# A norm, local-attention and shifted-MLP kernel on one core: p in bands of 32 queries by 48 keys, two weight loads on another queue, and a new operation order

## The chip, the cores and the metric

The kernel runs on one core of a Trainium2 chip. Its engines run side by side, each through its own list of instructions, and wait for one another by semaphores: TensorE (PE in the profile; its weight loads are listed as PEld), VectorE (DVE), ScalarE (ACT), GpSimd (POOL) and SyncE (SP). SP issues nearly all DMA transfers, and in this kernel it does little else. The metric is the device time of one execution in microseconds (us).

## The reference

x is 2048 tokens by 448 channels in bf16. The first half is attention with a window: 16 heads of 28 channels, and each query sees 8 keys, those at distance 0, 2, 4, ... 14 behind it.

```python
idx = pos[:, None] - off[None, :]          # off = 0, 2, ..., 14
logits = einsum("bhsd,bhswd->bhsw", q, k[idx]) * scale   # masked where idx < 0
attn = softmax(logits)
o = einsum("bhsw,bhswd->bhsd", attn, v[idx])
h = x + (o reshaped to 2048 x 448) @ wo    # q, k, v from layernorm(x) @ wqkv
```

The second half takes y = LN(h), where LN stands for layernorm: g = gelu(LN(y) @ w1); the four quarters of g's channels are shifted by -1, +1, -2 and +2 tokens; x1 = y + shifted @ w2. The output is h + x1 + gelu(LN(x1) @ w3) @ w4, where w3 is 448 x 1792 and w4 is 1792 x 448.

## The kernel before, in words

**Tiles.** The 2048 tokens are worked in four blocks t of 512 tokens for the attention and the first part of the MLP, and then in five units of 2, 4, 4, 4 and 2 tiles of 128 tokens (UNITS, L855) for the rest. The phases of a block are:

- N1 and A1: layernorm of x, the transpose of the normalised tokens into actT (channels on partitions), and the matmuls for q and k. PSUM (the tile ps) is copied to SBUF, to the tile arena.
- V: v by matmuls, copied to vt. Then DMA copies on SP build vw, the windows of v: each window is a range of 64 keys and the 16 before them, 80 rows, since a band of 64 queries reaches 14 keys back. The 16 columns of padding and the overlap are why vw is a second copy.
- A2: the products of q with each of its 8 keys, on DVE, into qk_r (128 x 4096, and 128 x 2048 for the last channels). TensorE sums them over each head's channels by matmuls with a matrix of ones, zc.
- Softmax: maximum (mx), difference (ls), exponential, sum, and the product pb, all of it on DVE and ACT. Two bands of the exponentials' 8 keys stand 80 columns apart in pb, and TensorE turns pb (matmuls with ident) into pt, keys on partitions.
- A3 (L781): for each il (128 queries) DVE spreads pt over a band matrix bd_r by a multiplication with a mask of zeros and ones (bmask), 80 partitions by 2048. TensorE multiplies it with vw: 32 matmuls per il, one for each head and half, whose weights are 80 rows by 32 columns of vw and whose moving side is 64 columns of bd_r. They lie in four column groups of the array (j). The result is copied to actT. Then follow the matmuls with wo and the residual.
- B1: the layernorm, a transpose of lntm into actT by DMA (an instruction DMA_TRANSPOSE on SP), the matmuls with w1, gelu.

Per unit there follow B2 (w2 and the residual, by scalar_tensor_tensor into arena), a layernorm with a DMA transpose, W3 (14 pairs of matmul sums with gelu into h3T) and B3 (w4, and the store).

**Order.** The program is first recorded as some 860 numbered operations. The table ORDER (L19) is one sequence of them all: each engine gets its operations in the order of this table, and buffers (pools bank, ln, act, qk, bd, h3) are handed out along it. The table OTHER (L50) lists the operations that go to their second choice of engine: a copy from ACT to DVE, or the product pb from DVE to POOL. `arrange` (L191) also keeps the two kinds of DMA apart: a DMA transpose waits for every plain copy that stands ahead of it in the sequence and behind the last transpose, and a plain copy waits for the transposes ahead of it. So SP's list is made of groups: copies, a transpose, copies, a transpose. All instructions are emitted from one line (L986 before; L1032 after), so the profile tells them apart by the names of their tiles: `actT<-lntm` on SP is a DMA transpose, `vw<-vt` a window copy.

**Loads.** x comes in seven transfers, the weights of q and k in two of 448 KB (load_rows, L426, into arena), v's in two of 224 KB, w3 in two of 896 KB, and w4 in two of 784 KB (L941). w4 takes the arena's place of wqkv, and so can be loaded only when TensorE has made the last use of wqkv. wqkv's and x's loads are the first things on SP's list.

Of the kernel before, what the change touches and what calls it, by code (L numbers as in the profile page):

```python
# [6 lines left out]
ALU = mybir.AluOpType  # L7
AX = mybir.AxisListType
# [40 lines left out]
"""  # L49
OTHER = """  # L50
92 102 187 188 381 493 499 502 505 549 550
"""
FULL = (4,)
FILL = (0, 0, 0, 0)
# [226 lines left out]
def bass_sequential_preLN__sliding_local_dilated__mixer_s_mlp__prompt_kernel(  # L281
# [7 lines left out]
    NTL = SEQ // 128  # L289
    NF = F // 128  # L290
    PADK = 16
    KW = 80
    KVW = PADK + 512
    SCALE = float(DH) ** -0.5
    EPS = 1e-5
    x2 = A_x.rearrange("b s d -> (b s) d")
    o2 = out.rearrange("b s d -> (b s) d")
    S = _Sched()
# [729 lines left out]
```

## Time and profile before

| | us |
|---|---|
| three runs | 192.14, 193.64, 194.31 |
| median | 193.64 |
| span of the profiled execution | 189.9 |
| median of the runs less that span | 3.7 |
| PE busy | 178.4 (94%), 2434 matmuls |
| DVE busy | 127.4 (67%), 226 instructions |
| ACT busy | 126.5 (67%), 295 instructions |
| POOL busy | 26.9 (14%) |
| DMA | 17.96 MB, 39.7% of 16 engines' span |

The span is the profiled execution's time from its first instruction to its last. The page gives no other time for that execution; what lies around the span (the launch and the end) is read from the runs, whose median is 3.7 us above it. PE's busy time is modelled from starts, so "busy" there doesn't mean that the array runs at its peak. The TensorE clock that was granted is 1.00 in every stretch.

### The profile page before, as it was taken

To read this page: it belongs to the slowest core of one execution; us is meant where nothing else is said; L and a number is where in the kernel's file an instruction comes from. 1 tells how busy PE (TensorE), PEld (TensorE's weight loads), DVE (VectorE), ACT (ScalarE), POOL (GpSimd) and SP (SyncE) were. 2 spreads that over 40 slices of the span, in tenths; PEclk is the share of its full clock that TensorE was granted. 3 is DMA by queue.
4 is the path that set the end of the run, shared out by engine and by line. 5 is a ranking of instruction groups with operands and counts; after the bars stand their busy time and mean duration, and the time that the engine had idled before them with its cause. 6 is when DMAs were issued, how large, how long until landed. Compare 5 with 4: busy or idle time off the path is not lost.

```text
span 189.9 us, 5626 instructions
## 1 busy us (share of the span) xinstructions
PE 178.4 (94%) x2434; PEld 107.5 (57%) x2434; DVE 127.4 (67%) x226; ACT 126.5 (67%) x295; POOL 26.9 (14%) x62
## 2 busy tenths in 40 slices
PE   6799989999988668999999999999999999999994
PEld 2494334545443434486544666666545664699973
DVE  6799999999999999897795337673973024001322
ACT  3569999999998999977698677049167004740330
POOL 2340000000002100202910000008026304000000
DMA  5993065554961553663534200518008202300202
GB/s 138 358 281 85 16 112 128 114 131 102 308 202 28 96 114 93 136 159 88 114 66 85 53 3 0 106 34 183 4 0 91 23 0 77 79 3 0 74 28 73
DMA packets 33217, 17.96 MB, mean 95 GB/s; under 512 B 21944, under 2 KB 32680, under 8 KB 33192
## 3 DMA queue, kind: packets, MB, share of 16 engines
q1 hardware_dynamic: 33192, 17.60, 39.7%
q8 instruction: 19, 0.31, 0.7%
q14 instruction: 6, 0.05, 0.1%
HBM read 7.91 MB, written 1.84 MB: 51 GB/s over the span
## 4 chain that ended last, share of the span: by engine, by line
PE 62%; DVE 17%; ACT 11%; DMA 6%; SPq 1%; issue 1%
PE ps L986 62%; DVE qk_r L986 9%; ACT arena L986 3%; DMA xin<-in_A_x_dram 3%; DMA actT<-lntm 3%; DVE bd_r L986 3%; ACT lntm L986 3%; ACT actT L986 2%; ACT vt L986 2%; DVE lntm L986 1%; DVE mx L986 1%; DVE st L986 1%; SPq L986 1%; ACT xin L986 1%; DVE pb L986 1%
## 5 line engine op out<-in xcount | busy, mean ns | idle before, releaser
L986 PE MATMUL ps<-actT,arena 64*128 64x512 bf16 (+1 forms) x756 | 68.8, 329 | 1.3 <-ACT vt L986 1.0
L986 PEld LDWEIGHTS ps<-actT,arena 64*128 64x128 bf16 x756 | 38.6, 94 | 27.3 <-ACT vt L986 2.6
L986 ACT ACTIVATE h3T<-ps 128x512 bf16<-128x512 f32 (+1 forms) x70 | 31.1, 515 | 33.7 <-PE ps L986 33.0
L986 PE MATMUL ps<-arena,h3T 64*128 64x448 bf16 (+2 forms) x434 | 44.5, 343 | 0.0
L986 PEld LDWEIGHTS ps<-arena,h3T 64*128 64x128 bf16 (+1 forms) x434 | 31.2, 94 | 11.5 <-ACT h3T L986 0.2
L986 DVE SCALAR_TENSOR_TENSOR qk_r<-ps,mrs,arena 128x448 bf16<-128x448 f32 (+1 forms) x17 | 10.6, 652 | 40.3 <-PE ps L986 33.2
L986 ACT ACTIVATE arena<-ps 128x512 bf16<-128x512 f32 (+6 forms) x73 | 32.8, 495 | 5.2 <-PE ps L986 4.6
L986 DVE TENSOR_TENSOR qk_r<-arena 128x4096 bf16<-128x4096 bf16 (+1 forms) x16 | 31.9, 2016 | 0.3 <-ACT arena L986 0.3
L986 POOL TENSOR_TENSOR arena<-arena,xin 128x448 f32<-128x448 f32 x16 | 16.7, 1066 | 43.5 <-DVE lntm L986 43.5
L986 DVE TENSOR_TENSOR bd_r<-arena,bmask 80x2048 bf16<-80x2048 bf16 x16 | 19.1, 1216 | 0.2 <-ACT arena L986 0.2
L986 PE MATMUL ps<-actT,w_s 64*112 64x512 bf16 x112 | 13.6, 378 | 2.2 <-DMA actT<-lntm 2.2
L986 PE MATMUL ps<-wo_s,actT 64*128 64x448 bf16 x128 | 14.8, 350 | 0.8 <-issue 0.5
L986 PE MATMUL ps<-w_s,arena 64*128 64x448 bf16 (+1 forms) x128 | 13.9, 350 | 1.0 <-ACT arena L986 1.0
L986 DVE SCALAR_TENSOR_TENSOR arena<-xin,rs_y,ps 128x448 f32<-128x448 bf16 x16 | 10.3, 676 | 4.0 <-PE ps L986 3.9
L986 PE MATMUL ps<-arena,actT 64*128 64x448 bf16 x112 | 12.5, 350 | 0.1
L986 ACT ACTIVATE lntm<-xin,nm 128x448 bf16<-128x448 bf16 x16 | 10.6, 685 | 2.2 <-DVE nm L986 2.0
L986 ACT ACTIVATE rs_x<-mv,epsilon 128x4 f32<-128x4 f32 (+2 forms) x16 | 4.9, 306 | 10.7 <-DVE mv L986 10.5
L986 ACT ACTIVATE actT<-ps 128x512 bf16<-128x512 f32 (+2 forms) x18 | 10.9, 644 | 1.4 <-PE ps L986 1.2
L986 PEld LDWEIGHTS ps<-actT,w_s 64*112 64x112 bf16 x112 | 7.7, 127 | 7.2 <-ACT arena L986 1.6
L986 PEld LDWEIGHTS ps<-w_s,arena 64*128 64x128 bf16 (+1 forms) x128 | 7.2, 94 | 6.1 <-ACT arena L986 1.1
L986 DVE BATCH_NORM_STATS2 st<-xin 128x6 f32<-128x448 bf16 x16 | 9.1, 616 | 1.7 <-DMA xin<-in_A_x_dram 1.4
L986 PEld LDWEIGHTS ps<-wo_s,actT 64*128 64x128 bf16 x128 | 6.2, 94 | 6.0 <-issue 0.9
(72 smaller groups left out, 156.6 us busy)
## 6 DMA issues: line engine op xcount, KB each, us to landing
arena<-in_B_w_dram SPq DMA_DIRECT2D x2, 896.0 KB, 8.1
out_dram<-qk_r SPq DMA_DIRECT2D x15, 112.0 KB, 1.9
arena<-in_B_w_dram SPq DMA_DIRECT2D x2, 784.0 KB, 5.2
vw<-vt SPq DMA_DIRECT2D x4, 320.0 KB, 5.7
vw<-vt SPq DMA_DIRECT2D x4, 256.0 KB, 3.9
arena<-in_A_wqkv_dram SPq DMA_DIRECT2D x2, 448.0 KB, 4.6
xin<-in_A_x_dram SPq DMA_DIRECT2D x2, 448.0 KB, 8.5
xin<-in_A_x_dram SPq DMA_DIRECT2D x3, 224.0 KB, 6.0
```

The source lines that it names most:

```text
L986: inst = getattr(eng, meth)(**kw)
```

## The change

1. **Bands.** With NARROW = (0, 1, 2, 3), all four blocks use bands of 32 queries by 48 keys. The mask is nmask (112 partitions, 16 columns), the product of the softmax is pn (windows 128 columns apart), the turn writes 112 rows: 48 keys of one half window, 16 rows unused, and 48 keys of the other half. bd_r is 112 partitions by 1024 for each il in place of 80 by 2048. The matmuls with vw become 64 per il in place of 32; each has 48 rows by 32 columns of weights and 32 moving columns, in two row groups and four column groups of the array, and writes one of two PSUM banks. Two il share the two banks, and two copies per pair of il bring them to actT (16 copies in all, as before).
2. **Windows of v.** vw has 128 partitions, and each block needs vwa (128 KB), vwd, vwb and vwe (192 KB each), vwc (48 KB) and vwp (16 KB, not for block 0): 768 KB in six copies, where it was 640 KB in four. In all 23 copies stand where 15 stood.
3. **Weights.** The two 448 KB loads of q's and k's weights are issued by ACT's queue instead of SP's. w3 is loaded in four pieces of 448 KB, and w4 in four (458, 458, 344 and 344 KB).
4. **Order.** ORDER is a new sequence throughout, and OTHER has 21 entries instead of 11. On the ACT engine 16 loads of an activation table stand where there were 12.

```diff
 FULL = (4,)
+NARROW = (0, 1, 2, 3)
...
-        load_rows("wqk", wqkv_s[:, :, 0:2 * D], A_wqkv, 0, 2 * D)
+        load_rows("wqk", wqkv_s[:, :, 0:2 * D], A_wqkv, 0, 2 * D, "act")
...
-        load_rows("w3", w3_s, B_w3, 0, F)
+        for q in range(2):
+            load_rows("w3%d" % q, w3_s[:, :, q * 896:q * 896 + 896], B_w3, q * 896, 896)
...
+            if narrow:
+                dma("vwa%d" % sl, vw[PADK:NK, sl, 0:8:2, :], vt[0:32, sl, :, :], 32 * 4096)
+                dma("vwd%d" % sl, vw[64:64 + NK, sl, 0:8:2, :], vt[16:64, sl, :, :], NK * 4096)
+                dma("vwb%d" % sl, vw[0:NK, sl, 1:8:2, :], vt[48:96, sl, :, :], NK * 4096)
+                dma("vwe%d" % sl, vw[64:64 + NK, sl, 1:8:2, :], vt[80:128, sl, :, :], NK * 4096)
...
+            if t in NARROW:
+                for pair in ((0, 1), (2, 3)):
+                    X = [_Tile(P_bank), _Tile(P_bank)]
+                    for at, il in enumerate(pair):
+                        bd = _Tile(P_bd)
+                        dve("tensor_tensor", block=True, out=bd(lambda v: v[0:64 + NK, 0:1024].rearrange("p (n g r) -> p n g r", g=4, r=NW)),
...
+                        S.group("pe", [("matmul", dict(out=X[h](lambda v, j=j, lo=256 * at + 64 * c + 32 * a2: v[32 * j:32 * j + 32, lo:lo + 32]),
+                                                       lhsT=vw[64 * h:64 * h + NK, sl, 2 * il + a2, (4 * c + j) * 32:(4 * c + j) * 32 + 32],
+                                                       rhs=bd(lambda v, h=h, lo=(16 * a2 + 4 * c + j) * 32: v[64 * h:64 * h + NK, lo:lo + 32]), start=True, stop=True))
+                                       for c in range(4) for a2 in range(2) for j in range(4) for h in range(2)],
...
-            for f in range(0, NF, 7):
-                dma("w4%d" % f, w4_s[:, f:f + 7, :], w4_v[:, f:f + 7, :], 128 * 7 * D * 2)
+            for f, n in ((0, 4), (4, 4), (8, 3), (11, 3)):
+                dma("w4%d" % f, w4_s[:, f:f + n, :], w4_v[:, f:f + n, :], 128 * n * D * 2)
```

What the new sequence moves is seen in the lists of the engines. First, the start of ACT's list. rs_x and rs_y are the two steps of the layernorm's factor for the first tiles, and mx there is a dummy exponential; rs_x waits for DVE's statistics. Before:

```order
L981 ACT_TABLE_LOAD
L986 ACTIVATE rs_x<-mv,epsilon 128x1
L986 ACTIVATE rs_y<-rs_x 128x1
L986 ACTIVATE rs_x<-mv,epsilon 128x1
L986 ACTIVATE rs_y<-rs_x 128x1
L986 ACTIVATE rs_x<-mv,epsilon 128x2
L986 ACTIVATE rs_y<-rs_x 128x2
L986 ACTIVATE actT<-ps 128x512 x3
```

After:

```order
L1027 ACT_TABLE_LOAD
L1032 ACTIVATE rs_x<-mv,epsilon 128x1 x2
L1032 ACTIVATE mx<-epsilon 128x1
L1032 DMA arena<-in_A_wqkv_dram 128x2x896
L1032 ACTIVATE rs_y<-rs_x 128x1 x2
L1032 ACTIVATE rs_x<-mv,epsilon 128x2
L1032 ACTIVATE rs_y<-rs_x 128x2
L1032 DMA arena<-in_A_wqkv_dram 128x2x896
L1032 ACTIVATE actT<-ps 128x512 x2
```

The first weight load now stands behind two activations that wait for statistics, the second behind three more and one more wait.

Second, SP's list where the transposes of blocks 2 and 3 and of the MLP's first block lie (`w_s` is w2, the 1792-column load is w3, the 7x448 one w4). Before:

```order
L986 DMA_TRANSPOSE actT<-lntm 128x16x128
L986 DMA vw<-vt 64x4x512
L986 DMA vw<-vt 16x512
L986 DMA vw<-vt 80x4x512
L986 DMA_TRANSPOSE actT<-lntm 128x16x128
L986 DMA vw<-vt 16x3x512
L986 DMA vw<-vt 80x4x512
L986 DMA vw<-vt 64x4x512 x2
L986 DMA w_s<-in_B_w_dram 112x4x448
L986 DMA vw<-vt 16x512
L986 DMA arena<-in_B_w_dram 128x2x1792 x2
L986 DMA vw<-vt 80x4x512
```

After:

```order
L1032 DMA vw<-vt 48x4x512 x2
L1032 DMA_TRANSPOSE actT<-lntm 128x16x128 x3
L1032 DMA arena<-in_B_w_dram 128x2x896
L1032 DMA vw<-vt 48x4x512 x2
L1032 DMA vw<-vt 16x512
L1032 DMA vw<-vt 32x4x512
L1032 DMA vw<-vt 16x3x512
L1032 DMA vw<-vt 48x4x512
L1032 DMA vw<-vt 32x4x512
L1032 DMA vw<-vt 48x4x512
L1032 DMA arena<-in_B_w_dram 128x2x896
L1032 DMA_TRANSPOSE actT<-lntm 128x8x128
```

Three transposes now stand in one row with no copy between, and behind them eight window copies and two pieces of w3 ahead of the transpose of the first unit (128x8x128).

Third, DVE's list at the place of which the prediction speaks: the rows with arena<-xin,rs_y,ps are B2's residual, qk_r<-ps,mrs,arena is the end of a unit (its store comes out of there), CAST actT<-ps a copy that ACT made before. Before:

```order
L986 TENSOR_TENSOR qk_r<-arena 128x2048
L986 TENSOR_SCALAR lntm<-arena,nm,rs_y 128x512
L986 SCALAR_TENSOR_TENSOR xin,mv<-ps,xin 128x448 x2
L986 TENSOR_TENSOR bd_r<-arena,bmask 80x2048
L986 TENSOR_SCALAR nm<-mv 128x4
L986 SCALAR_TENSOR_TENSOR arena<-xin,rs_y,ps 128x448 x4
L986 TENSOR_REDUCE mx<-ps 128x64
```

After:

```order
L1032 TENSOR_SCALAR rs_x<-mv 128x4
L1032 TENSOR_TENSOR bd_r<-arena,nmask 112x1024
L1032 CAST actT<-ps 128x16x32
L1032 SCALAR_TENSOR_TENSOR qk_r<-ps,mrs,arena 128x448
L1032 TENSOR_SCALAR lntm<-arena,mv,rs_y 128x512 x4
L1032 CAST actT<-ps 128x16x32
L1032 SCALAR_TENSOR_TENSOR qk_r<-ps,mrs,arena 128x448
L1032 SCALAR_TENSOR_TENSOR xin,mv<-ps,xin 128x448 x4
```

Before, the last four bd_r of block 3 stand behind this place; now all sixteen stand ahead of it, and the first store of a unit too.

More of the change, by code (lines that the diff above doesn't have):

```diff
@@ L292, in bass_sequential_preLN__sliding_local_dilated__mixer_s_mlp__prompt_kernel @@
     KW = 80
+    NK = 48
+    wide = [t for t in range(NST) if t not in NARROW]
     KVW = PADK + 512
@@ L365, in bass_sequential_preLN__sliding_local_dilated__mixer_s_mlp__prompt_kernel @@
         kr = [arv(A_KV + t * KVB + 3 * KVW, 128, 4 * KW).rearrange("p (j n) -> p j n", j=4) for t in range(NST)]
-        pt = [arv(A_KV + t * KVB + 4 * KVW, KW, 1024) for t in range(NST)]
+        pt = [arv(A_KV + t * KVB + 4 * KVW, 64 + NK if t in NARROW else KW, 1024) for t in range(NST)]
         maskrow = arv(A_KV + (NST - 1) * KVB, 1, 512)
@@ L601, in setup, with parities @@
         def setup():
-            par = ls[0:KW, 0, 128:168].bitcast(BF16).rearrange("p (e j) -> p e j", e=2)
-            pool("memset", ap=par, constant=0.0)
-            pool("affine_select", out=par, in_=par, pattern=[[1, 2], [2, KW // 2]], compare_op=ALU.not_equal, fill=1.0, base=0, channel_multiplier=-1)
-            for e in range(2):
-                dve("tensor_reduce", out=bmask[:].rearrange("p (m e r) -> p m e r", m=4, e=2)[:, :, e, :],
-                    in_=bass.AP(par.tensor, par.offset + e * (KW // 2) + 1, [list(par.ap[0]), [8, 4], [1, NW], [1, 8]]), axis=AX.X, op=ALU.max)
+            def parities(mask, parts, at, n, bases):
+                par = ls[0:parts, 0, at:at + n].bitcast(BF16).rearrange("p (e j) -> p e j", e=2)
+                pool("memset", ap=par, constant=0.0)
+                for base in bases:
+                    pool("affine_select", out=par, in_=par, pattern=[[1, 2], [2, n]], compare_op=ALU.not_equal, fill=1.0, base=base, channel_multiplier=-1)
+                m = (n - NW) // 8
+                for e in range(2):
+                    dve("tensor_reduce", out=mask[:].rearrange("p (m e r) -> p m e r", m=m, e=2)[:, :, e, :],
+                        in_=bass.AP(par.tensor, par.offset + e * n + 1, [list(par.ap[0]), [8, m], [1, NW], [1, 8]]), axis=AX.X, op=ALU.max)
+            if wide:
+                parities(bmask, KW, 128, KW // 2, (0,))
+            if NARROW:
+                parities(nmask, 64 + NK, 128 + KW // 2, NK // 2, (0, 64))
             pool("memset", ap=indj, constant=1.0)
@@ L765, in phase_A2 @@
             act(zs[:, sl, :], zs[:, sl, :], ACT.Exp, scale=-1.0)
-            row = lambda v, off, step: bass.AP(v, off, [[v.shape[1] * v.shape[2], 128], [step, NW], [16, 4], [DIL, NW], [1, DIL]])
-            mult = dict(out=row(pb, sl * NW * KW + DIL, KW + DIL), in0=row(ls, sl * 512, 64),
+            narrow = t in NARROW
+            if narrow:
+                kw, nr = 128, 64 + NK
+                out_p = bass.AP(pn, sl * NW * 128 + DIL, [[NSM * NW * 128, 128], [128 + DIL, NW], [64, 2], [1, 32]])
+            else:
+                kw, nr = KW, KW
+                out_p = bass.AP(pb, sl * NW * KW + DIL, [[NSM * NW * KW, 128], [KW + DIL, NW], [32, 2], [1, 32]])
+            src = pn if narrow else pb
+            mult = dict(out=out_p, in0=bass.AP(ls, sl * 512, [[NSM * 512, 128], [64, NW], [16, 4], [DIL, NW], [1, DIL]]),
                         in1=bass.AP(zs, sl * 64, [[64 * NSM, 128], [8, NW], [2, 4], [0, NW], [1, DIL]]), op=ALU.mult)
```

60 lines of the change are left out of this document (36 added, 24 removed), and 58 rows, old and new, of the table ORDER.

## The prediction, written before the result was known

> **What bounds the kernel now.** I read the time stretch by stretch first (columns: length; busy us and count of PE, PEld, DVE, ACT, POOL; clock, DMA share, GB/s).
>
> ```profile
> 8.25:20.00 11.75, 11.67 (x186) 8.23 (x188) 10.81 (x24) 9.74 (x28) 3.28 (x23) 1.00 0.72 187
> 20.00:40.00 20.00, 18.92 (x255) 8.39 (x251) 19.70 (x24) 19.66 (x56) 0.00 (x0) 1.00 0.46 90
> 40.00:60.00 20.00, 18.66 (x414) 9.43 (x412) 19.93 (x21) 19.26 (x51) 0.00 (x0) 1.00 0.64 175
> 60.00:82.00 22.00, 18.30 (x314) 9.73 (x310) 20.24 (x35) 20.11 (x42) 2.93 (x4) 1.00 0.47 100
> 82.00:187.37 105.37, 105.25 (x1254) 69.39 (x1250) 49.80 (x108) 54.21 (x116) 18.86 (x22) 1.00 0.28 58
> ```
>
> There are two kernels in this one. From 20 to 60 us DVE works 39.63 of 40 us and ACT 38.92; PE is the one that waits. From 82 us on PE is busy 105.25 of 105.37 us and the two others half the time. The chain that ended last says the same, and also gives DVE's pace free of gaps, since its pieces follow each other (start, length).
>
> ```profile
> 30.88 2.20 DVE qk_r L986
> 33.08 0.60 DVE pb L986
> 35.88 1.13 DVE bd_r L986
> 37.01 1.14 DVE qk_r L986
> 67.10 5.92 DMA actT<-lntm
> 73.07 35.45 PE ps L986 x583
> 108.60 78.75 PE ps L986 x820
> ```
>
> So a gain has one form: PE must reach its unbroken stretch with less work left. Behind the turning point nothing but PE's own work counts. What PE has to do is nearly the same before and after, and how long it needs where nothing holds it is read from three runs of equal matmuls.
>
> ```profile
> 134.90 9.67 PE L986 MATMUL ps<-actT,arena 64*128 64x512 bf16 x88
> 144.59 10.60 PE L986 MATMUL ps<-arena,h3T 64*128 64x448 bf16 x110
> 81.95 2.24 PE L986 MATMUL ps<-actT,arena 64*128 64x256 bf16 x38
> ```
>
> From start to start, with the last one's own latency (0.38, 0.35, 0.27 us) taken off: 0.107, 0.094 and 0.053 us each. By these prices all of PE's matmuls behind the warm-up make 167 us; it had 187.4 - 8.25 = 179.1. Some 12 us were lost, and that is the most that any reordering can bring.
>
> **The turning point moves.** The turn lies where DVE's list, run without a gap, is furthest behind PE's list. I sum both lists up to that place. Before, it is the four residuals of B2's second unit; they end at 83:
>
> ```profile
> 80.94 2.48 DVE L986 SCALAR_TENSOR_TENSOR arena<-xin,rs_y,ps 128x448 f32<-128x448 bf16 x4 [0.99 <-PE ps L986]
> ```
>
> DVE's work up to the third of them, at 82.4, is 77.0 us by the gap-free prices, PE's 63.0: DVE must start 14.0 us "ahead". After, the place is the copy actT<-ps behind the last bd_r of block 3, much further down both lists. What DVE has more up to there, counted from the two orders:
>
> - bd_r: 12 of 80x2048 by 1.13 = 13.6 become 16 of 112x1024. No row shows that shape. These rows (mean ns of one) bound it:
>
> ```profile
> L986 DVE TENSOR_TENSOR qk_r<-arena 128x4096 bf16<-128x4096 bf16 x12 | 27.1, 2282 | 0.3 <-ACT arena L986 0.3
> L986 DVE TENSOR_TENSOR bd_r<-arena,bmask 80x2048 bf16<-80x2048 bf16 x16 | 19.1, 1216 | 0.2 <-ACT arena L986 0.2
> L986 DVE TENSOR_TENSOR qk_r<-arena 128x2048 bf16<-128x2048 bf16 x4 | 4.9, 1217 | 0.0
> ```
>
> 80 and 128 partitions cost the same (1216, 1217), and 2048 elements more cost 1065 ns, 0.52 ns each, so 1024 fewer save 0.53: 1.13 - 0.53 = 0.60 us, an estimate (bounds 0.57, half, and 0.68, the busy time of the 512-element softmax steps). 16 x 0.60 = 9.6: **-4.0**.
> - The fourth block's softmax: 11 steps become 16, by 0.60 (pb above): +3.0.
> - Twelve copies out of PSUM that ACT made, or that lay later: five of actT by 0.60, two of vt and one of xin by 0.58, two arena by 0.66, two of half length by 0.33: +6.7, with one more of bf16 by 0.33: +7.1.
> - Ten more normalisations of 512 (0.32, or 0.46 from f32): +3.8. Four more residual sums and a first store: +2.3. Four statistics by 0.61: +2.4. Small ones: +0.4.
>
> Together +15.0, so 92.0 us. PE's list up to there has 89 more matmuls of 256 (by 0.0545: 4.9), 33 of wo and 8 of w2 and 56 of w4 (by 0.0945: 9.2), 28 of w1 (by 0.108: 3.0), the bands and turns 1.2: 18.3 more, 81.3 us. DVE's lead falls from 14.0 to 10.7: **-3.3 us**. The same sum for ACT shows its lead over PE falling by 3 as well. That is so although ACT has four more table loads
>
> ```profile
> L981 ACT ACT_TABLE_LOAD x6 | 7.7, 1283 | 0.9 <-PEq L1013 0.8
> L986 ACT ACTIVATE actT<-ps 128x512 bf16<-128x512 f32 x13 | 7.4, 594 | 0.9 <-PE ps L986 0.7
> ```
>
> by 1.28 = 5.1 us: ten copies of about 0.5 leave it for DVE. ACT's sum stays where it was (124 us), so the change doesn't hand the bound from DVE to ACT.
>
> **DVE's idle time up to the turn.** Before it is 82.4 - 77.0 = 5.4: 2.7 of start, the rest waits for PE, ACT and a transpose. The new order puts the first qk_r ahead of eight statistics that stood before it, so some of the 2.7 can go, while the place lies 15 us further on and collects more waits. Bounds -1.5 and +0.5, and I take **-0.4**.
>
> **The start.** Both weight loads go to ACT's list.
>
> ```profile
> 2.20 0.47 SPq L986
> 2.71 0.47 SPq L986
> 3.22 6.02 DMA xin<-in_A_x_dram
> 8.25 0.94 PE L986 MATMUL ps<-actT,arena 64*128 64x256 bf16 x14
> 4.88 0.29 ACT L986 ACTIVATE rs_x<-mv,epsilon 128x1 f32<-128x1 f32 x1 [0.58 <-DVE mv L986]
> 6.76 0.20 ACT L986 ACTIVATE rs_y<-rs_x 128x2 f32<-128x2 f32 x1
> arena<-in_A_wqkv_dram SPq DMA_DIRECT2D x2, 448.0 KB, 4.6
> ```
>
> SP issued them at 2.20 and 2.71; they landed after 4.6 (median), and x4, issued at 3.22, landed 6.02 later, where DVE waited for it. PE began A1 at 8.25. In the new list the first load stands behind the second rs_x, which ran at 4.88, the second behind the third rs_y, which ran at 6.76. Nothing in the trace shows an ACT DMA, so there are two ends. If a queued activation does not hold the DMA behind it, the loads leave at about 2.1 to 3, after the table load, beside more of x, and cost 0 to 1. If it does, the second load leaves at 7.0 and lands at 11.6, PE starts 3.3 later, and DVE's first qk_r, moved forward in its list, 2.6 later. x4 lands about a microsecond earlier in both, which DVE can use. I take **+0.4**, near the first end, as DVE's statistics fill the wait. [...]
>
> **The matmuls with the bands.** 512 become 1024, each with half the moving columns, in eight array tiles instead of four.
>
> ```profile
> 104.43 1.16 PEld L986 LDWEIGHTS ps<-bd_r,vw 80*32 80x32 bf16 x128 [0.42 <-issue]
> 52.45:52.70 0.25, 0.25 (x32) 1.00 1.01 358
> 104.43:105.65 1.22, 1.22 (x128) 1.00 0.81 194
> ```
>
> A burst of 32 takes 0.25 us: eight rounds of four tiles, 31 ns a round, 7.8 ns a matmul. 128 in one piece take 1.22, 9.5 ns each. There the weight loads lie as close as the matmuls (128 in 1.16 us), so I read it as the pace at which pairs of load and matmul are handed over, whatever a tile could do. Before, 12 short bursts and the long one make 4.2 us. After, 16 bursts of 64 at 7.8 to 9.5 ns a matmul make 8.0 to 9.7: +3.8 to +5.5 of PE's time. At the other end, eight tiles with half the columns take half of 0.25 per burst, 2.0 in all: -2.2. What is ahead of the turn is hidden while PE waits for DVE; but 16 copies and the wo matmuls wait for the bursts (0.5 to 0.6 us for 0.25 by 12), so some of it reaches DVE and ACT. I take **+1.0**, nearest to the hidden case, bounds -2.2 and +3.8. [...]
>
> **The sum** against the profiled execution: -3.3 - 0.4 + 0.4 + 1.0 = -2.3, a span of 187.6. The median of the runs lies 3.7 above the span of before, so **191.3 us**, 1.2% under 193.64. (About 1%, 1.9 us, is what a measurement of this kernel can tell from no change: 191.7 and 195.6 are the bounds.)
>
> **Rivals.**
>
> (a) Slower: **the copies between the transposes.** A transpose waits for every copy ahead of it, and now four transposes have more ahead of them.
>
> ```profile
> vw<-vt SPq DMA_DIRECT2D x4, 320.0 KB, 5.7
> vw<-vt SPq DMA_DIRECT2D x4, 256.0 KB, 3.9
> actT<-lntm SPq DMA_TRANSPOSE x11, 4.4
> SPq L984 <- DMA vw<-vt: 11.8, 4, 5.2
> PE ps L986 <- DMA actT<-lntm: 2.2, 2, 1.5
> ```
>
> SP waited 11.8 us for window copies already, PE only 2.2 for a transpose: the slack took the rest. The new order has three transposes in a row, then eight copies and two pieces of w3 before B2's first transpose; w4's pieces, which need PE to be through with wqkv, stand before those of B1's blocks 2 and 3, and the second unit's is a tie too. Comparing when each can be issued with when its reader is due I find slacks of -1 to +1.5 us. Six issues by 0.47 instead of four add 0.9 per block, and a window set that lands 1.3 later (5.7 against 4.4) makes each of four transposes late by that: 4 x 1.3 = +5.2, a span of 192.8, **196.5 us**. It decides when a block's windows need over some 5.5 us from the first issue to the last landing instead of about 4. For it: PE's waits are 2.2 with more slack. Against: the windows are smaller pieces over more partitions. Chance 0.31.
>
> (b) The ACT list holds the DMAs: +2.6 in place of +0.4: **193.5**. Chance 0.10.
>
> (c) The bands are paid in full: +3.8 in place of +1.0: **194.1**. Chance 0.08.
>
> (d) The new order fills the gaps as well: idle -1.5, bands 0, start 0: 189.9 - 4.8 + 3.7 = **188.8**. Chance 0.16.
>
> The forecast, 191.3 with its own range of 189.9 to 192.7, has 0.35, of which 0.24 lies under 191.7. Faster 0.16 + 0.24 = 0.40; same 0.11 + 0.10 + 0.08 = 0.29; slower 0.31. The range reaches to (d) and to (a) with half a microsecond for its unknown price: 188.5 to 197.0.
>
> **What the profile would show.** If the turning point moved as said, PE's last unbroken piece of the chain begins near 95 us with 90 us behind it. bd_r should read 112x1024 at 0.65 to 0.70 busy. The first A1 matmul stands at 8 to 9 (b: over 11). Bursts of 64 take 0.5 us (lower end: 0.12). Under (a) PE's waits for `actT<-lntm` rise from 2.2 to over 5 and SP's for `vw<-vt` over 15. I am wrong if DVE has gaps beyond 6 us before the last bd_r, or if PE waits for it behind that.

## The result, and the profile after

| | before | after |
|---|---|---|
| median of four runs | 193.27 us | 217.40 us |
| ratio, 95% interval | | 1.1295 [1.1202, 1.1388] |
| span of the profiled execution | 189.9 | 214.7 |
| mean granted clock in it | 1.000 | 0.952 |

The change makes the kernel 13% slower. (The ratio and its interval are worked out from the fast runs, not from the two medians.) The prediction was 191.3 us with a range up to 197.0, so it was far off. The list of what PE waited for in the changed kernel (total, times, longest) has two entries that the kernel before did not have at that size; the third row is the kernel before:

```profile
PE ps L1032 <- issue: 11.3, 6, 3.2
PE ps L1032 <- DMA arena<-in_A_wqkv_dram: 6.2, 1, 6.2
PE ps L986 <- issue: 0.5, 1, 0.5
```

The chain that ended last shows where (start, length):

```profile
6.40 7.49 DMA arena<-in_A_wqkv_dram
13.98 6.69 PE ps L1032 x78
...
37.68 2.65 issue
40.33 2.78 PE ps L1032 x91
...
71.46 2.11 issue
...
76.09 1.30 issue
...
88.58 1.25 issue
89.83 1.41 PE ps L1032 x127
91.23 3.24 issue
94.48 16.27 PE ps L1032 x182
...
123.57 0.81 issue
124.38 87.84 PE ps L1032 x950
```

Six times the chain stands at "issue" for 0.8 us or more: PE waits for nothing that the profile shows. The timeline of PE at the first of them shows that it is no semaphore, since the halt lies inside one burst of 64 matmuls on the same tiles, 13 before its end:

```profile
36.58 1.10 PE L1032 MATMUL ps<-bd_r,vw 48*32 48x32 bf16 x115
40.33 0.23 PE L1032 MATMUL ps<-bd_r,vw 48*32 48x32 bf16 x13 [2.65 <-issue]
```

The table by stretches (length; busy us and count of PE, PEld, DVE, ACT, POOL; clock, DMA share, GB/s) shows the third thing that is new, the clock:

```profile
13.98:17.95 3.97, 3.97 (x38) 3.27 (x40) 0.00 (x0) 0.00 (x0) 3.81 (x26) 0.50 1.13 222
37.68:40.33 2.65, 0.00 (x2) 0.00 (x0) 0.00 (x0) 0.00 (x0) 0.00 (x0) 1.00 0.10 22
41.90:45.35 3.45, 3.39 (x18) 1.03 (x16) 3.45 (x5) 3.33 (x11) 0.00 (x0) 0.51 0.53 98
88.58:94.48 5.90, 1.41 (x130) 1.27 (x129) 0.69 (x1) 0.60 (x1) 0.00 (x0) 0.59 0.49 92
94.48:99.60 5.12, 5.12 (x44) 2.17 (x45) 3.12 (x3) 4.64 (x8) 0.00 (x0) 0.50 0.77 204
```

PE works at half clock (0.50) around three of its waits: the one for the weights, the halt at 37.68, and the pair of halts at 88.58 and 91.23. Around the halts at 71.46, 76.09 and 123.57 the clock stays at 1.00. In the trace the clock is 0.50 from 11.14 to 17.97, 41.86 to 45.27 and 89.65 to 99.89, and PE is at work in 4.0, 3.4 and 6.8 us of these: some 14 us. At 0.50 half of that is lost, which is my estimate.

So the 24.8 us between the spans come apart as follows: 5.7 at the start (the first A1 matmul at 13.98 instead of 8.25), 10.8 at "issue" (11.3 less 0.5 before), about 7.1 by the clock. That makes 23.6, if none of it is hidden behind other work; the rest is not assigned.

DVE's products did become as short as the prediction said. The rows of the band work in the changed kernel (busy us, mean ns | idle before it):

```profile
L1032 DVE TENSOR_TENSOR bd_r<-arena,nmask 112x1024 bf16<-112x1024 bf16 x16 | 10.2, 682 | 0.1
L1032 PE MATMUL ps<-bd_r,vw 48*32 48x32 bf16 x1024 | 10.6, 184 | 9.8 <-issue 9.2 <-ACT h3T L1032 0.5
```

### The profile page after: what moved, and what is told of

It reads as the page before. It is cut to its first block, busy times and chain, and to the rows that moved or that the text cites. A ratio compares the mean times of both kernels' runs of the same rounds, so it can differ in the third digit from the quotient of the medians.

```text
span 214.7 us, 6682 instructions
## 1 busy us (share of the span) xinstructions
PE 189.7 (88%) x2946; PEld 106.6 (50%) x2946; DVE 125.3 (58%) x238; ACT 126.6 (59%) x288; POOL 25.4 (12%) x62
## 4 chain that ended last, share of the span: by engine, by line
PE 71%; ACT 14%; issue 6%; DMA 4%; DVE 3%
PE ps L1032 71%; ACT arena L1032 6%; DMA arena<-in_A_wqkv_dram 3%; ACT lntm L1032 2%; ACT vt L1032 2%; DVE st L1032 1%; ACT L1032 1%; ACT xin L1032 1%; DMA xin<-in_A_x_dram 1%; ACT actT L1032 1%; DVE pn L1032 1%; ACT ls L1032 1%; ACT rs_x L1032 0%; DVE mx L1032 0%; ACT h3T L1032 0%
## 5 line engine op out<-in xcount | busy, mean ns | idle before, releaser
L1032 PE MATMUL ps<-actT,arena 64*128 64x512 bf16 (+1 forms) x756 | 73.1, 340 | 6.3 <-DMA arena<-in_A_wqkv_dram 6.2
L1032 ACT ACTIVATE arena<-ps 112x512 bf16<-112x512 f32 (+5 forms) x70 | 31.8, 493 | 12.1 <-PE ps L1032 11.0
L1032 PEld LDWEIGHTS ps<-arena,h3T 64*128 64x128 bf16 (+1 forms) x434 | 24.6, 94 | 17.3 <-PE ps L1032 0.5
L1032 DVE SCALAR_TENSOR_TENSOR qk_r<-ps,mrs,arena 128x448 bf16<-128x448 f32 (+1 forms) x17 | 10.8, 651 | 35.8 <-PE ps L1032 35.7
L1032 ACT ACTIVATE actT<-ps 128x512 bf16<-128x512 f32 (+2 forms) x15 | 9.5, 652 | 18.1 <-PE ps L1032 17.9
L1032 PE MATMUL ps<-bd_r,vw 48*32 48x32 bf16 x1024 | 10.6, 184 | 9.8 <-issue 9.2
L1032 PE MATMUL ps<-wo_s,actT 64*128 64x448 bf16 x128 | 17.4, 407 | 0.0
L1032 PE MATMUL ps<-arena,actT 64*128 64x448 bf16 x112 | 13.7, 350 | 3.0 <-issue 2.1
L1032 PEld LDWEIGHTS ps<-bd_r,vw 48*32 48x32 bf16 x1024 | 9.2, 90 | 13.1 <-issue 9.9
L1032 DVE SCALAR_TENSOR_TENSOR arena<-xin,rs_y,ps 128x448 f32<-128x448 bf16 x16 | 10.4, 674 | 7.7 <-PE ps L1032 7.5
L1032 DVE TENSOR_SCALAR lntm<-arena,mv,rs_y 128x512 bf16<-128x512 f32 x14 | 7.5, 591 | 9.9 <-ACT rs_y L1032 7.9
L1032 ACT ACTIVATE lntm<-xin,nm 128x448 bf16<-128x448 bf16 x16 | 10.6, 669 | 3.1 <-DVE nm L1032 3.1
L1032 POOL TENSOR_TENSOR mrs<-nm,rs_y 128x4 f32<-128x4 f32 x4 | 0.8, 198 | 85.8 <-ACT rs_y L1032 85.8
```

The lines of the kernel that those rows point to most:

```text
L1032: inst = getattr(eng, meth)(**kw)
```

## The two theories

**H, held loads.** The timeline of ACT at the start:

```profile
4.82 0.29 ACT L1032 ACTIVATE rs_x<-mv,epsilon 128x1 f32<-128x1 f32 x1 [2.73 <-DVE mv L1032]
4.82 0.43 ACTq L1032 DMA_DIRECT2D arena<-in_A_wqkv_dram  x1
5.02 0.28 ACT L1032 ACTIVATE rs_x<-mv,epsilon 128x1 f32<-128x1 f32 x1
5.20 0.19 ACT L1032 ACTIVATE mx<-epsilon 128x1 f32<-128x1 f32 x1
...
6.39 0.20 ACT L1032 ACTIVATE rs_y<-rs_x 128x2 f32<-128x2 f32 x1
6.40 0.37 ACTq L1032 DMA_DIRECT2D arena<-in_A_wqkv_dram  x1
```

Neither load waits for a semaphore itself. The first leaves within 10 ns of the start of the first rs_x, the second within 10 ns of the start of rs_y, and both of these activations wait for a semaphore. The second rs_x and mx (5.02 and 5.20) stand ahead of the first load as well, but have no more to wait for, and the load left before they began. So in this trace it is the wait of an activation, and not its work, that holds the DMAs behind it.

**S, supply of instructions.** The page lists a DMA queue of the kind "instruction" (q8) with 23 transfers after (0.38 MB, 16 KB each in the trace) and 19 before. PE has 5946 and 4914 instructions, 23.2 and 19.2 times 256, so I read these transfers as the fetches of PE's list, in blocks of 256. I numbered PE's instructions in the trace (loads, matmuls and the few that only wait for a semaphore): the six halts stand behind numbers 961, 1985, 2241, 2753, 3009 and 4033, and each is a multiple of 256 less 63. At each, a 16 KB transfer ended 1.25 to 1.44 us before PE went on. The table is worked out from the trace's records, with "begins" counted from the moment at which PE enters the block ahead. That a fetch can begin from that moment on, as an expectation below has it ("could be asked for"), was my estimate and is not shown: in the two traces other fetches began from 1.6 us before such a moment to 3.6 us behind it.

```
            block     fetch of the next   fetch    PE goes  PE stood
kernel ends  lasts     block begins after  ends at  on at    still
after   961  1.94 us   2.49 us              38.98    40.33   2.83 us
after  1985  2.35      2.56                 72.23    73.56   2.45
after  2241  2.35      1.20                 76.14    77.39   1.48
after  2753  2.46      1.63                 88.52    89.83   1.43
after  3009  1.21      2.33                 93.04    94.48   3.44
after  4033  3.84      2.35                123.06   124.38   0.99
before 1729  4.36      2.54                 56.70    58.14   0.86
before 3265  3.53      1.58                107.12   108.60   0.45
```

A block and the halt behind it make 3.8 to 5.2 us in every row: with a late fetch more, with a prompt one less. A burst of 64 matmuls is 128 instructions with its weight loads, and two bursts are a block that is gone in 1.2 us. The blocks without a halt last 4 to 13 us, but for one of 2.97 in the changed kernel whose successor was fetched 0.41 us after it began; that one was just in time.

The rivals: **T**, the halts belong to the eight small tiles in the array; **C**, the copies ahead of the transposes, the prediction's rival (a), or another fault of the new order; **D**, the prediction's price of the bands, their hand-over at most. The kernel before was measured again beside every run, with medians from 191.5 to 194.1 us, so each ratio is taken against the kernel before beside that run.

## The experiments

**The loads at the head of ACT's list.**

```diff
-... rs_x, rs_x, mx, DMA wqka, rs_y, rs_y, rs_x, rs_y, DMA wqkb, ...
+mx, DMA wqka, DMA wqkb, ... rs_x, rs_x, rs_y, rs_y, rs_x, rs_y, ...
```

> The changed kernel with one edit: the two loads of q's and k's weights stand at the head of ACT's list, ahead of every activation that waits. Theory H (a DMA in ACT's list is held while an activation ahead of it waits): the loads leave before 3 us instead of at 4.82 and 6.40, the first A1 matmul stands at 8 to 9.5 instead of 13.98, the clock stays at 1.00 from 8 to 20, and the time falls by 5.5 to 8 us, to 209 to 212. Rival (ACT's queue is slow in itself, 7.0 us to landing against 4.6 on SP): the start moves to 10 to 11 only, and the time falls by 3 or less. The waits of PE for 'issue', 11.3 us, stay.

Measured: 211.92 us, ratio 1.0995 [1.0909, 1.1082], 5.5 us (3.0 points of the ratio) under the changed kernel, as H said. The two loads left at 0.94 and 1.41 and landed after 4.3 us (median) instead of 7.0, which speaks for H and against a slow queue. Two signs did not come: the first A1 matmul came at 10.43 and not at 8 to 9.5, and the clock was 0.50 from 8.61 to 12.03. Ahead of x's tiles the loads delayed x (the first rs_x at 5.93 instead of 4.82). The place is what counts, and this one is too early. The halts stayed, 11.0 us, at the same six numbers.

**The loads on SP in their old place.**

```diff
-        load_rows("wqk", wqkv_s[:, :, 0:2 * D], A_wqkv, 0, 2 * D, "act")
+        load_rows("wqk", wqkv_s[:, :, 0:2 * D], A_wqkv, 0, 2 * D)
```

> The changed kernel with one edit: the two weight loads on SP's queue in their old place. Theory H: PE's first A1 matmul at 8 to 9 instead of 13.98 and the clock 1.00 there, so 5.5 to 7.5 us less than the changed kernel, 209 to 212; the stalls of 11 us stay at the same instruction numbers. If the start is hidden behind DVE's and ACT's work, less than 3 us.

Measured: 208.12 us, ratio 1.0825 [1.0718, 1.0931], 9.3 us (4.7 points of the ratio) less than the changed kernel, more than the 5.5 to 7.5 expected. The first A1 matmul, from PE's timeline:

```profile
8.17 4.00 PE L1040 MATMUL ps<-actT,arena 64*128 64x256 bf16 x70 [0.34 <-DVE actT L1040]
```

It is 5.8 us earlier, and the clock stays at 1.00 until 34. The loads on ACT's queue thus cost their whole delay and the clock's fall on top (2.0 us, half of the 4.0 in which PE worked at half clock there). The halts are at five of the six numbers, 10.4 us: behind 4033 there is none, and the fetch concerned began 0.84 us after PE entered the block ahead instead of 2.35.

**The old bands in the new order.** All blocks with bands of 64 by 80; window copies and operations in the same number, so that the order stays.

```diff
-NARROW = (0, 1, 2, 3)
+NARROW = ()
...
-                dma("vwa%d" % sl, vw[PADK:KW, sl, 0:8:2, :], vt[0:64, sl, :, :], 64 * 4096)
-                dma("vwb%d" % sl, vw[0:KW, sl, 1:8:2, :], vt[48:128, sl, :, :], 80 * 4096)
+                dma("vwa%d" % sl, vw[PADK:NK, sl, 0:8:2, :], vt[0:32, sl, :, :], 32 * 4096)
+                dma("vwd%d" % sl, vw[NK:KW, sl, 0:8:2, :], vt[32:64, sl, :, :], 32 * 4096)
+                dma("vwb%d" % sl, vw[0:NK, sl, 1:8:2, :], vt[48:96, sl, :, :], NK * 4096)
+                dma("vwe%d" % sl, vw[NK:KW, sl, 1:8:2, :], vt[96:128, sl, :, :], 32 * 4096)
...
```

> The changed kernel with its order, its loads and as many window copies, but bands of 64 queries by 80 keys in all blocks: 512 matmuls with bands instead of 1024, 16 products of 80x2048 on DVE. Theory S (PE runs out of instructions: the bursts use them up faster than they are brought): the 11.3 us of 'issue' fall under 2, the clock's falls after 30 us go, and the time is 200 to 205, although DVE has 8.5 us more to do. Rival C (rival a of the prediction, copies ahead of transposes, or the new order itself): the time stays over 212 and PE waits elsewhere.

Measured: 206.03 us, ratio 1.0673 [1.0579, 1.0767]. "issue" is gone from PE's waits altogether (from 11.3 us), and the clock falls at the start and once more, from 84.9 to 91.8, after PE waited 1.04 and 1.22 us for DVE. The time is a microsecond above the 200 to 205 that S said, far under the 212 of C.

**The old bands, and the loads first.** Both edits.

> Both edits, so that the new order, w3 and w4 in pieces and the other copies on DVE are what is left of the change. S and H together: no 'issue' waits, start at 8 to 9.5, clock 1.00 throughout. DVE has 16 x 0.53 = 8.5 us more than in the changed kernel up to the turn, so by the sum of the prediction 193 - 3.3 + 8.5, 197 to 199. If the new order hides this work, 193 to 195. Rival C: over 203.

Measured: 200.43 us, ratio 1.0408 [1.0342, 1.0475], clock 1.00 throughout the profile. What PE waits for now:

```profile
PE ps L1047 <- DVE bd_r L1047: 4.2, 8, 1.0
PE ps L1047 <- DVE lntm L1047: 2.3, 1, 2.3
PE ps L1047 <- DVE actT L1047: 2.0, 3, 1.2
...
PE ps L1047 <- DMA actT<-lntm: 0.8, 1, 0.8
```

It waits for DVE, which has 8.5 us more to do here, and hardly for a transpose. The late start (first A1 matmul at 10.62 instead of 8 to 9.5) is as large as the excess over the expected 197 to 199. C, which said over 203, is out for this kernel: PE waits under a microsecond for SP's groups of copies and transposes.

**The bands in the old order.** The kernel before with the bands alone; its sequence is kept, but the two bursts of a pair stand together, 128 matmuls.

In words:

```diff
-NARROW absent, 4 x (bd_r 80x2048, 32 matmuls, copy) per block
+NARROW = (0, 1, 2, 3), 2 x (2 bd_r 112x1024, 2 x 64 matmuls, 2 copies) per block
```

> The kernel before with its order and loads and only the bands of 32 by 48 put in (the two bursts of a pair of il stand together, 128 matmuls, and the two copies behind them). Theory S: PE runs dry of instructions in most of the eight bursts, 'issue' waits of 8 to 14 us, the clock falls after some of them, 202 to 212. Rival D (the prediction's: bands cost their hand-over at most, and DVE saves 8.5): 188 to 195, 'issue' under 2.

Measured: 209.13 us, ratio 1.0779 [1.0648, 1.0911]. D said 188 to 195, S 202 to 212. PE's list of waits begins:

```profile
PE ps L1039 <- issue: 7.7, 5, 2.5
```

The halts stand behind 1217, 1985, 2241 and 4033, again multiples of 256 less 63, in another order with another content. The cause moves with the bands, not with the order.

**Twice as many instructions and nothing else.** The kernel before, each band matmul issued twice.

```diff
-                     for c in range(4) for a2 in range(2) for j in range(4)])
+                     for _ in range(2) for c in range(4) for a2 in range(2) for j in range(4)])
```

> The kernel before with each of its 512 matmuls with bands issued twice, the second time with the same operands to the same place: nothing else is added, no engine but PE has more to do, and no burst has smaller tiles. Theory S (PE's list comes in blocks of 256 instructions; a block must last about 3.8 us, 4.8 with busy DMA queues, or PE runs dry at its end): PE stands still inside or right behind a burst and always at an instruction whose number is a multiple of 256 less 63 (961, 1985, ... as in the changed kernel), by the lengths of the blocks in the trace of before in about five places (1473, 1985, 2241, 4033, 4289), 6 to 11 us in all; the time is 198 to 206. Rival T (the stalls belong to eight small tiles in the array, which this kernel does not have): no stalls, 4 us more of PE's time, of which a part is hidden: 193 to 197.

Measured: 200.77 us, ratio 1.0459 [1.0367, 1.0550]. There are no eight tiles here, and yet:

```profile
PE ps L993 <- issue: 5.5, 4, 2.6
```

In the records PE halts behind 961 (0.75 us), 1985 (2.24), 2241 (1.07) and 4033 (2.79): 6.9 us, at three of the five places named and at one more. T is out: four tiles do it too.

**The control.** The kernel before with one matmul of 512 columns ahead of each burst.

```diff
+                mms([(b(), ident[:], bass.AP(ident, 0, [[128, 128], [0, 4], [1, 128]]), True, True, 512, None)] +
...
```

> The control to the run with doubled matmuls: the kernel before with one matmul of 128x128 by 512 columns ahead of each of its 16 bursts, to the same PSUM bank, which the burst then overwrites. It adds about as much PE time per burst (0.22 to 0.43 us) with 2 instructions instead of 64. Theory S: no new stalls beyond the two of before, 193 to 197. If PE's time around the bursts is what costs, and not the number of instructions, the time is that of the doubled matmuls.

Measured: 196.92 us, ratio 1.0224 [1.0148, 1.0300]. No new halt; the one behind 1729 stays (0.57). So more PE time at the bursts costs about 2.2% by itself, which I had priced as mostly hidden. In the profile up to 1.7 us of this is the clock, 0.50 from 67.10 to 70.51, after PE had waited 1.6 us for ACT. By the difference, the instructions in the doubled run cost the other half of its 4.6%.

**The changed kernel with half the instructions for the bands.** Each two matmuls of 32 columns made one of 64 with the first window's weights, the loads on SP. The second half of the windows is left out of the result.

```diff
-  64 matmuls per il: lhsT vw[.., 2 * il + a2, ..], 32 columns of bd_r
+  32 matmuls per il: lhsT vw[.., 2 * il, ..], the 2 x 32 columns of both a2
```

> The changed kernel with the two weight loads on SP's queue in their old place behind the first four tiles of x, and with each two matmuls of 32 columns of a band (the two windows of an il) made one of 64 columns with the first window's weights; so the second half of the windows of v is left out of the result. Order, DVE's products of 112x1024, copies and loads stay; PE has half the instructions for the bands and the same columns. If S and H are all that the prediction missed, this is what it described: no 'issue' stalls, start at 8 to 9, clock 1.00, 190 to 194. If the order has a fault of its own (rival C), 196 to 200, as DVE has no longer the 8.5 us of the wide products that the run with the order alone had.

Measured: 191.55 us, ratio 0.9980 [0.9938, 1.0023]. This is the kernel that the prediction described, without the hand-over of 512 more matmuls and without the loads on ACT's queue. From its chain (ACT without a tile's name is a load of an activation table):

```profile
27.72 5.00 DMA vw<-vt
32.73 5.35 DMA actT<-lntm
...
85.57 1.28 ACT L1040
86.86 1.21 ACT h3T L1040 x4
88.09 1.28 ACT L1035
89.38 0.64 ACT ls L1040
90.05 0.69 DVE mx L1040
90.73 0.59 DVE arena L1040
91.34 0.70 DVE pn L1040
92.09 94.41 PE ps L1040 x1096
```

The turn lies at 92 us with 94 us behind it (the prediction said near 95 and 90). "issue" is 0.6 (one halt, behind 2241), the clock 1.00. Added up over its pieces ahead of the turn, the chain stands on ACT for 33.7 us and on DVE for 14.5, and six table loads are in it (7.7 us); in the kernel before, ahead of 73.07, it stands on ACT for 20.3 and on DVE for 32.4, with no table load. So where PE has to wait, it now waits at the end of ACT's work more than of DVE's.

To the run above with all the matmuls and the same start (208.12) it is 16.6 us: 9.8 is "issue" (10.4 less 0.6), and about 5.0 the clock, since PE worked 3.3 and 6.7 us at half clock in that run (34.13 to 37.54 and 81.92 to 92.16). The 1.8 left would be the price of the longer bursts.

**The same bands at half the instructions in the old order.**

```diff
-the bands of the old-order run, 64 matmuls per il
+the same with 32 per il, as in the run above
```

> The kernel before with its order and loads and the bands of 32 by 48 in all blocks, each two matmuls of 32 columns made one of 64 with the first window's weights (so the second half of the windows is left out of the result): 512 matmuls, 16 products of 112x1024, the instructions of before. It stands to the run with the whole bands in this order as a run without the supply of instructions as a limit. Theory S: the 7.7 us of 'issue' fall under 1.5 and the clock stays at 1.00; DVE has 8.5 us less than before, of which 6.4 lie ahead of the turn, so 186 to 190. If the bands are no gain in any order (since DVE's time is not what PE waits for), 191 to 194.

Measured: 194.50 us, ratio 1.0122 [1.0056, 1.0188]. I expected 186 to 190, and 191 to 194 if the bands were no gain in any order. The halts are gone and the clock is 1.00, as S said, but DVE's gain is not used. A stretch of this run, and the middle of its chain:

```profile
40.00:60.00 20.00, 17.18 (x426) 8.73 (x424) 14.63 (x18) 17.39 (x46) 0.00 (x0) 1.00 0.70 188
```

```profile
61.92 4.34 DMA actT<-lntm
66.28 2.15 DMA vw<-vt
68.44 6.00 DMA actT<-lntm
74.46 5.15 DMA arena<-in_B_w_dram
79.62 4.54 DMA actT<-lntm
```

DVE works 14.63 of 20 us where it worked 19.93, and from 61.9 to 84.2 the chain is SP's: transposes, a window copy and a weight load, one after the other. In the kernel before, of SP's transfers only the transpose at 67.10 stands in this place of the chain. Whether DVE is now ahead of SP's transfers, or the two more window copies of a block hold them up, this run does not separate.

**The bands in one block.** The old order, the whole bands in block 2 alone, and in block 1 alone: equal work and equal numbers of instructions in different places.

```diff
-NARROW = (0, 1, 2, 3)
+NARROW = (2,)        and        NARROW = (1,)
```

> The kernel before with its order and loads, and the whole bands (all 64 matmuls per il, the right result) in block 2 alone. By the lengths of the 256-instruction blocks in the trace of before, the added 256 instructions fall among long matmuls: one block gets as short as 3.5 us (ending at instruction 2753), so at most 1.3 us of a new stall. DVE saves 4 x 0.53 = 2.1 ahead of the turn. 189.5 to 192.5. If any use of the bands brings stalls like those of all four, 194 and more.

> The same in block 1 alone: as many matmuls, instructions, copies and DVE products as with block 2 alone. Here the bursts stand close together: two blocks of instructions get as short as 2.2 and 1.4 us, ending at instructions 1729 and 1985, so by the rule (3.8 to 4.8 us a block) two stalls of 1.6 to 2.6 and 2.4 to 3.4 us there, and after them a fall of the clock is likely. 194 to 199. If the place makes no difference, as with block 2.

Measured: block 2, 195.85 us, ratio 1.0123 [1.0023, 1.0223]; block 1, 198.20 us, ratio 1.0293 [1.0224, 1.0363]. Block 1 behaves as expected: halts behind 1729 (2.23 us) and 1985 (0.97, less than the 2.4 to 3.4 expected: behind the first halt the second's block lasted 2.76 us instead of 1.4). Block 2 has no halt behind 2753, as the rule allowed. Its time is in the range of the rival all the same (194 and more, where 189.5 to 192.5 was expected), and its runs spread from 192.99 us (mean clock 1.00) to 197.97. The profile is of the longest run, and there

```profile
PE ps L1039 <- issue: 4.1, 2, 2.7
```

has as its longest the halt of the kernel before behind 1729, 3.05 us in the records: the fetch began 5.07 us after PE entered the block ahead, with the DMA queues 0.71 busy. The bands of block 2 come behind it, so they don't use up this block's instructions. Why the fetch was later than in the kernel before isn't settled, and with it the time of this run stays open.

**Fetches without data traffic.** This asks whether a fetch waits behind data. The kernel before with the loads of w2 and w3 at 10.6 to 12.8 us instead of 44 to 48, where they run beside the block that ends at 1729.

```diff
-SP: ... w1, vwc, transpose, vw ..., w2, vwp, w3a, w3b, vwb, transpose ...
+SP: ... w1, w2, w3a, w3b, vwc, transpose, vw ..., vwp, vwb, transpose ...
```

> The kernel before with one edit: the loads of w2 and of w3 (392 KB and two of 896 KB) stand right behind w1's on SP's list, at 11 us, instead of at 44 to 48 us, where they move while PE runs the bursts of block 0 and 1. In the trace of before the instructions for the block that begins at 57.28 (instruction 1729) were fetched 2.54 us after they could be asked for, with the DMA queues 0.88 busy, and PE stood still 0.86 us; with block 2's bands the same fetch waited 5.07 us and PE 3.05. Theory Q (a fetch of instructions waits behind the data that is moving): without w3's traffic there the wait falls to 1.0 to 1.6 us as in the quiet stretches, the stall at 1729 goes, the clock stays at 1.00 in all runs, and the time is 189.5 to 192 with little spread. If a fetch is late for another reason, the stall stays, 192 to 195. What could be lost: the first DMA transpose has w3 ahead of it and may come up to 2 us later.

Measured: 194.35 us, ratio 1.0116 [1.0051, 1.0181]. The fetch began 0.61 us after PE entered the block ahead (2.54 before), with the queues idle, and the halt behind 1729 is gone. That is what Q says, in one pair of traces; two late fetches with idle queues (named at the end) show that traffic can't be the whole of it. The time did not fall to the 189.5 to 192 expected, for the price that was named, a transpose up to 2 us later, came out higher:

```profile
PE ps L993 <- DMA actT<-lntm: 3.5, 2, 2.9
```

The first transpose left 2.8 us later (25.77 instead of 22.95), PE stood still for 2.9 us from 27.4, and the clock was 0.50 from 31.5 to 34.9. No run beat the kernel before beyond its interval.

The kernels that differ in order, bands and the loads of wqk, against the kernel before:

| order | bands | loads of wqk | ratio |
|---|---|---|---|
| old | wide | SP | 1 |
| old | 32 by 48, half the instructions | SP | 1.012 |
| old | 32 by 48 | SP | 1.078 |
| new | wide | ACT, first | 1.041 |
| new | wide | ACT, as changed | 1.067 |
| new | 32 by 48, half the instructions | SP | 0.998 |
| new | 32 by 48 | SP | 1.083 |
| new | 32 by 48 | ACT, first | 1.100 |
| new | 32 by 48 | ACT, as changed | 1.130 |

## Why the prediction was wrong, step by step

**"The turning point moves", -3.3: right in its place, not in its gain.** With the two missed costs taken out the turn lies at 92 us with 94 us behind it, near the place forecast. The gain isn't there. This run has neither the hand-over (+1.0) nor the loads on ACT's queue (+0.4), so the sum leaves it -3.7 us, 1.9%. It has -0.2%, with an interval from -0.6% to +0.2%, and where the mean clock is 1.00 its nine runs and the six of the kernel before beside them both take 191.3 us on average. The step that failed is "the change doesn't hand the bound from DVE to ACT". The prediction compared whole sums, in which four more table loads (5.1 us) are made up for by ten copies that leave ACT. In the chain ahead of the turn ACT has 33.7 us where it had 20.3, DVE 14.5 where it had 32.4, and six table loads stand there where none did. What each of these is worth isn't separated. DVE's shorter products are of use in the new order, since with the wide ones its ratio is 1.041, of which some 2 us are a late start. The estimate of 0.60 us for a bd_r holds: its busy mean is 682 ns, against 1216 for the wide one, 0.53 less.

**Wrong: "The start", +0.4.** Rival (b) was what happened, and its price was too low as well. I had given it 0.10 and 2.6 us; it cost 5.7, and 2.0 more by the clock. The step that failed is the choice of the near end of the bounds. No run shows the term of +0.4; the runs showed a start 5.7 us later in its place. In the trace the loads left at 4.82 and 6.40, each at the start of an activation that waits for a semaphore, and with the loads first at 0.94 and 1.41, where none that waits for statistics was ahead. Two activations with nothing to wait for (5.02 and 5.20) did not hold the first load. The price was low because in the meantime SP went on with wo, w1, w2 and the first piece of w3 (issued from 5.32 to 11.05), and the DMA share was 1.06 to 1.13 from 7.80 to 17.95: the second load needed 7.5 us from its issue, not the 4.6 of before.

**Wrong: "The matmuls with the bands", +1.0 with an upper bound of +3.8.** I priced the hand-over of a pair and took PE's list as always there. The pace itself was right: a burst of 64 that isn't halted takes 0.47 to 0.57 us from its first matmul to its last, where 0.5 was forecast. (The working gave +3.8 to +5.5 for that, but the bound was set at +3.8.) The term that was missing is the supply: 11.3 us in six halts; with the clock's falls, and what the longer bursts cost besides, 16.6 us (208.12 against 191.55). It was not in any rival. The trace of before had it in small: "issue" of 0.51 us stood in its chain at 57.63, and PE stood still for 0.45 us at 108.14, at the end of the block that holds the burst of 128. The prediction gave a price to neither. The sentence that "what is ahead of the turn is hidden while PE waits for DVE" failed too: the control lost 2.2% by one long matmul per burst, so PE's time at the bursts is not hidden.

What the traces show of it: the halts stand to the instruction behind multiples of 256 less 63, a block and its halt make 3.8 to 5.2 us here, and blocks of 1.2 to 2.5 us left 1.4 to 3.4 us open.

**Missing: the clock.** No term and no rival had it, as the clock was 1.00 in every stretch of before. It cost about 7 us by the estimate above. In the trace the stretches at 0.50 last 6.83, 3.41 and 10.24 us, multiples of 3.41, and the fall at 41.86 came 1.53 us after a halt of 2.65 us.

The profiled execution of the kernel before was free of it, but others are not: its runs beside the doubled kernel have mean clocks of 1.00, 0.991 and 0.982, with averages of 191.3, 192.2 and 193.9 us. In every run on record the time is 1.7 to 1.8 us above the span of the same execution. So of the 3.7 us that the prediction added to its span, only these 1.7 lie around a span; the other 2 are what the median execution took more than the profiled one, as much as the clock makes in these runs.

**Rival (a), 0.31,** did not come about in the changed kernel: PE's list of waits there has no transpose (2.2 us before), and SP's wait for `vw<-vt` is 11.1 us where over 15 would have been the sign. Its price set a window copy's 5.7 us against a transpose's 4.4, two different transfers. The path exists: with half the instructions a window copy and a transpose stand in the chain from 27.72 to 38.08 in the new order, where PE waits 1.1 us for a transpose, and transposes hold it from 61.9 in the old one (1.012).

**Rivals (c) and (d).** Without the added hand-over and without the late start the ratio is 0.998, not the 0.975 of (d). (c), the full hand-over without halts, can't be seen alone, since the whole bands in all four blocks brought halts in every run.

## What to carry to other kernels

Count instructions per microsecond where a phase is broken into small matmuls: here 256 of PE's instructions (128 pairs of weight load and matmul) had to last about 4 to 5 us (3.8 to 5.2 with the halt), or PE stood still, and around the two longest halts (3.44 and 2.83 us) the clock fell to 0.50. An "issue" of half a microsecond inside a run of equal matmuls in the profile of before (0.51 at 57.63) was the warning, and doubling the burst's count in an unchanged kernel, beside a control with about as much PE time in few instructions, prices it (here 4.6% against 2.2%). A load that is moved to ACT's list should stand ahead of everything there that waits, and behind the loads that are needed first: on ACT's list the place alone made 5.5 us here. Sums of whole engines don't show which one bounds the stretch ahead of the turn; the chain does.

## What the hardware showed that I had not expected

PE's halts stood behind instruction 256k - 63 in all eleven traces with halts, whatever the order; the fetch before such a halt took 0.9 to 1.4 us and PE went on 1.2 to 1.5 us after its end. A fetch that made PE halt began 1.1 to 1.6 us after PE had entered the block ahead where the DMA queues were idle, and mostly 1.6 to 2.7 where they were busy (once 5.07, and five times 1.0 to 1.3; their share up to the fetch was 0.63 to 1.12 at the four late ones of this kind in the changed kernel, and 0.00 at the one of 1.20); taking the data away brought one of them from 2.54 to 0.61. Two fetches began late with idle queues, both for the block behind 4033 in the new order: 2.35 us in the changed kernel and 2.94 with the loads first on ACT's list. They have no explanation here.

An activation that waits for a semaphore held the DMA behind it in ACT's list until it could start, to within 10 ns.

The falls and rises of the clock lie on one grid of 3.41 us in each trace. Divided along this grid, the changed kernel's trace shows what stands ahead of a fall and what does not bring one (columns as above):

```profile
38.45:41.86 3.41, 1.53 (x87) 1.11 (x88) 1.21 (x3) 1.21 (x3) 0.00 (x0) 1.00 0.04 7
72.58:76.00 3.42, 2.44 (x127) 1.68 (x128) 1.75 (x4) 0.87 (x3) 1.73 (x2) 1.00 0.21 35
86.24:89.65 3.41, 1.82 (x127) 1.39 (x123) 1.93 (x6) 2.24 (x6) 0.00 (x0) 1.00 0.28 91
```

The first and the last of these are followed by a fall, the one between is not. In the changed kernel the pieces ahead of its three falls have PE busy for 0.06, 1.53 and 1.82 us, and no piece at full clock with 2.11 us or more has a fall behind it. Over all traces with a fall, 20 pieces with PE busy for up to 1.93 us of the 3.41 are followed by one, and none with 1.96 or more is; one piece with 1.79, in the doubled kernel, is not followed by one either. The clock came back behind pieces that were at least 89% busy. So here the place of a halt on the grid went with what it cost: the halt of 2.45 us behind 1985 lies across two pieces, with PE busy for 2.29 and 2.44 us of them, and no fall followed; the halt of 2.83 us behind 961 lies mostly in one, with 1.53, and a fall followed.
